# Attention with a local band, then a dense layer: the band mask moved from a product in SBUF to a sum in PSUM, with other joins, costs and a split last store

## The chip, the cores and the metric

The kernel runs on one core of one Trainium2 chip. The metric is the device time of one execution in microseconds (us), the median over several runs. An engine is named as in the profile: PE (TensorE, matmuls), PEld (its weight load, which overlaps PE), DVE (VectorE), ACT (ScalarE), POOL (GpSimd), SP (SyncE, which here only issues DMAs).

## The reference

Eight batches with eight heads, 576 positions, 64 features a head, all float32. Attention has two parts that are added, and its result, 4608 tokens by 512 features, goes through a dense layer with 2048 hidden units.

```python
q_d, k_d, v_d = means of q, k, v over 4 neighbouring positions   # 144 positions
out_up = repeat(softmax(q_d @ k_d.T / 8) @ v_d, 4)               # pooled part
mask = abs(pos[:, None] - pos[None, :]) < 4                      # local part: a band
scores = where(mask, q @ k.T / 8, -1e9)
attn_out = out_up + softmax(scores) @ v
x = attn_out as 4608 x 512
h = x @ w_in                                                     # 512 x 2048
out = (h - tanh(h)) @ w_out                                      # 2048 x 512
```

## The kernel before

**Pairs.** Attention is worked in 32 pairs p of two heads: batch b = p // 4, and j = p % 4 is the place of the pair's 128 features in x. For each pair the chain is:

1. Loads of q and k (`load_qk`, L401) and of v (`load_v`, L426) by SP's queue, into 4 buffers `qkn` and 5 buffers `vst`. A cast of v to bfloat16, `vw` (`prep_v`, L451), and of q and k, `qr` (L515 for p of 4 and more, L523 for the first four).
2. A transpose that brings the features to the partitions: by PE (L547) with copies from PSUM (L551) for pairs 0 to 11, by a DMA of SP (L531) with a copy by ACT (L534) from pair 12 on.
3. Sums over four positions for the pooled part: `half` (L564) and `qkd` (L569) for q and k; for v by matmuls (L492) for the first twelve pairs, by two POOL sums (L472, L476) after that.
4. Scores (L584), into PSUM. A query tile of 120 positions needs 128 keys, so the local scores are 2 heads x 480 columns in two banks, and 2 heads x 96 columns in two others beside the pooled scores (L606). The largest score is not subtracted.
5. Exponentials by ACT from PSUM into the bfloat16 tile `E` in SBUF: 960 columns (L622), 192 (L634), and the pooled 576 (L637).
6. The band. For pairs 0 to 3, PE adds it before the scores: a matmul of the identity with `bias` (L589), which is 0 inside the band and -32768 outside. From pair 4 on DVE multiplies `E` in place, after the exponential, with `mask`, which is 1 inside and 0 outside: 960 columns (L626) and 192 (L641). `mask` is built on POOL; `bias` is made from it by one DVE instruction (L813).
7. Outputs (`outs`, L650 and L657): matmuls of `E` with v, which has a column of ones, so that the sum of the weights comes with it. DVE takes the reciprocal (L670) and scales (L672) into `ln`.
8. Back to features on partitions, with the two parts added. For pairs 0 to 11, matmuls (`back`, L683 to L692) add and transpose at once, and one copy (L720 on DVE or L721 on ACT) gives `xT`. From pair 12 on a DMA of SP transposes `ln` into `lT` (L696), and a `join` of two additions (L703, L709) on DVE or POOL writes `xT`.

**The dense layer** takes 512 tokens at a time, nine blocks kb. `mm1` (L734): 16 x 4 matmuls of 512 columns; ACT takes tanh into `u` (L742) and DVE subtracts it from the PSUM bank into `gT` (L745). `mm2` (L760): 4 token tiles x 16 matmuls, ACT copies to `y` (L771), SP stores (L774). Block 0 does all of mm1, then all of mm2; block 1 does mm1; from block 2 on mm1(kb) alternates with mm2(kb - 1). The weights are loaded, with a cast, in four parts each by POOL's queue (L438 for w_in, L442 for w_out); part f of w_out serves mm2's fc from 4f to 4f + 3. "Dense starts" when x of the first batch, pairs 0 to 3, is there; block 1 needs pairs 4 to 7 too.

**The order.** All instructions are first recorded in class `Program` with a cost in ns. `choice` records one that may go to several engines. `order` (L109 to L222) then simulates the engines: it takes again and again the instruction that can start first, by priority where several can, with the costs given, the times `LAT` from the end of an instruction to its user on another engine, and the PSUM banks (`cap`: how many banks a kind may hold). The result is emitted as it is: each engine runs its list in that order. DMA costs of the simulation are `T_QK`, `T_V`, `T_W`. So a changed cost moves instructions between engines and places, far from the line that was edited. Matmuls of the dense layer fill PE wherever no attention work can run; a few idle fillers (L911) keep PE busy before the dense start.

Of the kernel before, what the change touches and what calls it, by code (L numbers as in the profile page):

```python
# [9 lines left out]
BF16 = mybir.dt.bfloat16  # L10
# [13 lines left out]
class Program:  # L24

    LAT = {"PE": 270, "ACT": 150, "DVE": 110, "POOL": 150, "SP": 50, "DMA": 2200}
    RING = 230

    def __init__(self):
# [8 lines left out]
        self.use = []  # L38
        self.toks = []
# [69 lines left out]
    def order(self):  # L109
# [56 lines left out]
        for i in range(n):  # L166
            if left[i] == 0:
                make_ready(i)
        for step in range(n):
            best = None  # L170
            for eng, cand in ready.items():
                if not cand:
                    continue
                now = max(free.get(eng, 0.0), min(at[i] for i in cand))
                if eng == "PE":
# [5 lines left out]
                elif eng == "DMA":  # L181
                    pick = min((turn.get(self.ring[i][0], -1), start[self.ring[i][1]], i)
                               for i in cand if at[i] <= now)[2]
                else:
                    pick = min((self.ops[i][4], i) for i in cand if at[i] <= now)[1]
# [12 lines left out]
            end = now + self.ops[i][1]  # L198
            want = [t for t in self.use[i] if t.first == i]
# [57 lines left out]
def kernel(  # L257
# [41 lines left out]
    mask = fixed("mask", [128, 576], BF16)  # L299
# [69 lines left out]
    def c_mask():  # L369

        GP.memset(mask, 1.0)
        m4 = mask[:, 0:480].rearrange("p (t c) -> p t c", c=QW)
        for part, pat in ((m4, [[0, 4], [1, QW]]),
                          (mask[:, 480:576], [[1, 96]])):
            neg = [[-s, n] for s, n in pat]
            GP.affine_select(
                out=part, in_=part, compare_op=ALU.is_ge, fill=0.0,
                base=-1, pattern=neg, channel_multiplier=1)
            GP.affine_select(
                out=part, in_=part, compare_op=ALU.is_ge, fill=0.0,  # L380
                base=7, pattern=pat, channel_multiplier=-1)
        GP.affine_select(
            out=mask[:, 0:QW], in_=mask[:, 0:QW], compare_op=ALU.is_ge,
            fill=0.0, base=-4, pattern=[[0, QW]], channel_multiplier=1)
        GP.affine_select(
            out=mask[:, 480:576], in_=mask[:, 480:576], compare_op=ALU.is_ge,
            fill=0.0, base=99, pattern=[[0, 96]], channel_multiplier=-1)
# [115 lines left out]
    def attention(p):  # L503
# [34 lines left out]
        else:  # L538
            for a0, a1, tn, cn in ((0, 5, 290, 740), (5, 9, 230, 620)):
# [10 lines left out]
                def copy(fn, a0=a0, a1=a1, b16=b16):  # L550
# [5 lines left out]
                          ("DVE", cn, lambda copy=copy: copy(V.tensor_copy))][:1 + (p < NP)],  # L556
# [10 lines left out]
        def add2(eng):  # L567
            with nc.allow_low_precision("pooled q and k"):
                eng.tensor_tensor(out=qkd[s][:, 0:G],  # L569
                                  in0=half[:, :, 0, :],  # L570
                                  in1=half[:, :, 1, :], op=ALU.add)
        P.choice([(name, n1, lambda eng=eng: add1(eng)) for name, n1, _, eng in adders],
# [48 lines left out]
        e3 = E[e][:, 1152:1728].rearrange("p (h c) -> p h c", h=2)  # L621
        op("ACT", 960, lambda: A.activation(  # L622
            out=e1, in_=two(t1)[:, :, 0:480], func=AF.Exp, scale=SCALE),
           drain=[t1], writes=[("E", e, 0)], pri=pri)
        if p >= NP:
            op("DVE", 950, lambda: V.tensor_tensor(  # L626
                out=e1, in0=e1,
                in1=mask[:, 0:480].unsqueeze(1).to_broadcast([128, 2, 480]),
                op=ALU.mult), reads=["mask"], writes=[("E", e, 0)], pri=pri)
        yield  # L630
        if not new:
            op("PE", 380 * cold + 100 * (p < NP), s2, slack=late, reads=qks + [("qkd", s)],
               fill=[t2], pri=pri)
        op("ACT", 310, lambda: A.activation(  # L634
# [5 lines left out]
        if p >= NP:  # L640
            op("DVE", 450, lambda: V.tensor_tensor(  # L641
                out=e2v, in0=e2v,
                in1=mask[:, 480:576].unsqueeze(1).to_broadcast([128, 2, 96]),
                op=ALU.mult), reads=["mask"], writes=[("E", e, 1)], pri=pri)
# [50 lines left out]
        if p >= X_DMA:  # L695
# [18 lines left out]
            P.choice([("DVE", 1900, lambda: join(V)), ("POOL", 1400, lambda: join(GP))],  # L714
# [37 lines left out]
    def mm2(kb, i):  # L752
        ts, part, g = i // 4, i % 4, kb % 2
        if part == 0:
            ycur[0] = P.psum(1, "d")
        tok = ycur[0]

        def mm(e):
            for fc in range(4 * part + 2 * e, 4 * part + 2 * e + 2):
                T.matmul(one(tok), gT[g][:, fc, ts * 128:ts * 128 + 128],  # L760
                         w_out_sb[:, fc, :],
                         start=(fc == 0), stop=(fc == N_FF - 1))
        for e in range(2):
            op("PE", 432, lambda e=e: mm(e),
               reads=[("w_out", part, c) for c in range(4)] +
# [179 lines left out]
```

The softmax here doesn't subtract the row's maximum and nothing guards it: scores larger than these inputs give would overflow.

## Time and profile before

| what | value |
|---|---|
| median of 13 runs | 333.79 us (332.4 to 336.17) |
| the profiled execution's own time | 333.7 us |
| its span in the profile | 331.7 us |
| granted clock of TensorE | 1.0 |
| busy: PE, DVE, ACT, POOL | 314.6, 213.2, 202.6, 176.7 us |
| first dense matmul, end of the last one | 25.8, 327.3 us |
| last store: issued, landed | 328.0, 330.05 us |
| a 512-column matmul, one to the next | 0.216 us |
| mask products, 28 + 28 | 32.0 + 16.0 us |
| joins: 9 on DVE, 11 on POOL | 19.8 us, 16.0 us |

The span is what the profile sees of one execution; the time of the execution is 2.0 us longer here. In a list of groups a row has the line, engine, operation, what it writes and reads with shapes, how often, the busy time in all and the mean of one in ns, and then the idle time before it and what ended that. "<-" in the waits names the instruction that released the waiting one. SPq and POOLq are the queues that issue DMAs.

| stretch, us | PE busy | DVE | ACT | POOL |
|---|---|---|---|---|
| 26 to 50 (24) | 22.5 | 19.1 | 17.7 | 11.4 |
| 50 to 100 (50) | 48.8 | 33.7 | 34.8 | 36.1 |
| 100 to 246 (146) | 141.2 | 115.8 | 101.7 | 110.6 |
| 246 to 312 (66) | 65.7 | 26.7 | 28.0 | 1.3 |

After 246 us only the dense layer is left.

### The profile page before, as it was taken

The numbers are of one execution on the slowest core, as the hardware profiler recorded it, in microseconds if no ns is written. First come the engines' busy times: TensorE is split into PE (matmuls) and PEld (weight loads), VectorE is DVE, ScalarE is ACT, GpSimd is POOL, SyncE is SP. The second block draws the span as 40 slices with busy tenths as digits, with TensorE's granted clock in tenths as the row PEclk, the third lists the DMA queues.
The fourth block names the chain that finished last, engine by engine and source line by source line (L and its number), as shares of the span: only waits on it lengthen the run. The fifth ranks groups of instructions, "written<-read, shape, count | busy, mean of one in ns | idle before, by whom it ended". The sixth has DMA issues, their size and how long they took to land.

```text
span 331.7 us, 6505 instructions
## 1 busy us (share of the span) xinstructions
PE 314.6 (95%) x2420; PEld 158.7 (48%) x2461; DVE 213.2 (64%) x330; ACT 202.6 (61%) x334; POOL 176.7 (53%) x211
## 2 busy tenths in 40 slices
PE   7889989999999999999899899999999999999994
PEld 2554445655444444445454345444444444444441
DVE  4877874478966969777979878758754334443300
ACT  3977854589778766687866466868534443344411
POOL 8564547768667698988988848787310000000000
PEclk9999999999999999999999999999999999999999
DMA  7999999999999999999999989982320001000121
GB/s 235 263 224 209 249 236 240 292 296 215 287 218 268 226 185 274 264 235 225 243 243 253 275 212 288 196 199 61 91 59 34 32 35 62 32 32 32 38 90 64
DMA packets 108862, 59.80 MB, mean 180 GB/s; under 512 B 86174, under 2 KB 96030, under 8 KB 108830
## 3 DMA queue, kind: packets, MB, share of 16 engines
q1 hardware_dynamic: 104318, 54.60, 70.7%
q0 software_dynamic: 4224, 4.19, 7.8%
q10 hardware_dynamic: 288, 0.59, 0.5%
q8 instruction: 19, 0.31, 0.4%
q14 instruction: 13, 0.11, 0.1%
HBM read 43.64 MB, written 9.44 MB: 160 GB/s over the span
## 4 chain that ended last, share of the span: by engine, by line
PE 70%; DVE 11%; DMA 9%; ACT 3%; POOL 2%; issue 2%; SPq 1%; POOLq 0%; ACTq 0%; DVEq 0%
PE bank L760 30%; PE bank L734 29%; DMA qkn<-in_k_dram 6%; PE bank L650 2%; DVE E L626 2%; DVE gT L745 2%; PE bank L584 2%; DVE ln L672 2%; PE bank L657 2%; DVE E L641 2%; DVE xT L709 1%; DMA v<-in_v_dram 1%; DMA lT<-ln 1%; ACT E L622 1%; DVE xT L703 1%
## 5 line engine op out<-in xcount | busy, mean ns | idle before, releaser
L734 PE MATMUL bank<-xT,w_in_sb 128*128 128x512 bf16 x557 | 143.7, 379 | 1.4 <-DVE gT L745 0.2
L760 PE MATMUL bank<-w_out_sb,gT 128*128 128x512 bf16 x555 | 141.6, 379 | 1.5 <-issue 0.6
L745 DVE TENSOR_TENSOR gT<-bank,u 128x512 bf16<-128x512 f32 x144 | 97.1, 685 | 62.3 <-ACT u L742 61.7
L742 ACT ACTIVATE u<-bank 128x512 f32<-128x512 f32 x144 | 86.0, 598 | 75.6 <-PE bank L734 74.0
L734 PEld LDWEIGHTS <-w_in_sb 128*128 128x128 bf16 x576 | 53.9, 98 | 62.0 <-issue 0.9
L760 PEld LDWEIGHTS <-gT 128*128 128x128 bf16 x576 | 53.9, 98 | 62.0
L564 POOL TENSOR_TENSOR half<-qk 128x576 f32<-128x576 bf16 x28 | 32.1, 1146 | 20.7 <-ACT qk L551 11.6
L626 DVE TENSOR_TENSOR E<-E,mask 128x960 bf16<-128x960 bf16 x28 | 32.0, 1143 | 12.0 <-ACT E L622 11.9
L622 ACT ACTIVATE E<-bank 128x960 bf16<-128x960 f32 x32 | 31.1, 972 | 12.3 <-PE bank L584 12.1
L515 POOL CAST qr<-qkn 128x1152 bf16<-128x1152 f32 x28 | 32.7, 1168 | 7.9 <-DMA qT<-qr 5.1
L672 DVE TENSOR_TENSOR ln<-bank,r 128x896 bf16<-128x896 f32 x32 | 34.7, 1086 | 0.9
L771 ACT COPY y<-bank 128x512 f32<-128x512 f32 x36 | 21.1, 586 | 19.9 <-PE bank L760 18.3
L451 POOL CAST vw<-vst 128x640 bf16<-128x640 f32 x31 | 25.7, 832 | 9.5 <-DMA vst<-in_v_dram 9.5
L472 POOL TENSOR_TENSOR v<-v 72x512 f32<-72x512 f32 x20 | 25.4, 1272 | 1.6 <-DMA v<-in_v_dram 0.8
L534 ACT COPY qk<-qT 128x1152 bf16<-128x1152 bf16 x20 | 24.1, 1207 | 1.7 <-DMA qT<-qr 1.7
L650 PE MATMUL bank<-vw,E 128*128 128x65 bf16 x320 | 19.8, 194 | 3.2 <-DVE E L641 2.3
L569 POOL TENSOR_TENSOR qkd<-half 128x288 bf16<-128x288 f32 x29 | 21.0, 724 | 1.5 <-DVE r L670 0.5
L476 POOL TENSOR_TENSOR vp<-v 72x256 bf16<-72x256 f32 x20 | 14.5, 725 | 13.6 <-PE bank L657 12.0
L650 PEld LDWEIGHTS <-E 128*128 128x128 bf16 x320 | 16.4, 98 | 10.1 <-DVE E L641 2.5
L637 ACT ACTIVATE E<-bank 128x576 bf16<-128x576 f32 x32 | 21.1, 661 | 0.0
L703 POOL TENSOR_TENSOR xT<-lT 128x480 bf16<-128x480 bf16 x11 | 11.3, 1026 | 14.2 <-DMA lT<-ln 14.1
L641 DVE TENSOR_TENSOR E<-E,mask 128x192 bf16<-128x192 bf16 x28 | 16.0, 571 | 0.8 <-ACT E L634 0.7
(75 smaller groups left out, 223.9 us busy)
## 6 DMA issues: line engine op xcount, KB each, us to landing
vst<-in_v_dram SPq DMA_DIRECT2D x62, 160.0 KB, 4.9
qkn<-in_q_dram SPq DMA_DIRECT2D x32, 288.0 KB, 5.3
out_dram<-y SPq DMA_DIRECT2D x36, 256.0 KB, 4.5
qkn<-in_k_dram SPq DMA_DIRECT2D x30, 288.0 KB, 6.0
v<-in_v_dram SPq DMA_DIRECT2D x20, 288.0 KB
w_in_sb<-in_moe_w_in_dram POOLq DMA_DIRECT2D x4, 512.0 KB, 12.6
w_out_sb<-in_moe_w_out_dram POOLq DMA_DIRECT2D x4, 512.0 KB, 10.8
qkn<-in_k_dram ACTq DMA_DIRECT2D x2, 288.0 KB, 3.4
```

Source lines behind the costliest of these rows:

```text
L451: P.choice([(eng, ns, lambda fn=fn: fn(out=vw[w][:, 2 * jj:2 * jj + 2, :, 0:64], in_=vst[s])) for eng, ns, fn in CAST_V[p >= NEARLY]], rea ...
L472: GP.tensor_tensor(out=v2, in0=v4[s][:, :, :, 0:128], in1=v4[s][:, :, :, 128:256], op=ALU.add)
L515: op("POOL", 1300, lambda: GP.tensor_copy(out=qr[s].rearrange("p a (h d) -> p h a d", h=2), in_=qkn[sn].rearrange("p h (a d) -> p h a d", ...
L564: eng.tensor_tensor(out=half, in0=four[:, :, 0:2, :], in1=four[:, :, 2:4, :], op=ALU.add)
L622: op("ACT", 960, lambda: A.activation(out=e1, in_=two(t1)[:, :, 0:480], func=AF.Exp, scale=SCALE), drain=[t1], writes=[("E", e, 0)], pri=pri)
L626: op("DVE", 950, lambda: V.tensor_tensor(out=e1, in0=e1, in1=mask[:, 0:480].unsqueeze(1).to_broadcast([128, 2, 480]), op=ALU.mult), reads= ...
L650: T.matmul(two(to)[:, hh, 65 * t:65 * t + 65], E[e][:, c:c + 128], vw[w][:, 2 * jj + hh, t, :], start=True, stop=True)
L672: op("DVE", 1060, lambda: V.tensor_tensor(out=ln[s].rearrange("p n (h d) -> p h n d", d=D), in0=blocks()[:, :, :, 0:64], in1=r[s].unsqueez ...
L734: T.matmul(one(tok), w_in_sb[:, dc, fc * 128:(fc + 1) * 128], xT[dc][:, kb * 512:kb * 512 + 512], start=(dc == 0), stop=(dc == N_DC - 1))
L742: op("ACT", 590, lambda: A.activation(out=u[us], in_=one(tok), func=AF.Tanh), drain=[tok], writes=[("u", us)], pri=DPRI)
L745: op("DVE", 670, lambda: V.tensor_tensor(out=gT[g][:, fc, :], in0=one(tok), in1=u[us], op=ALU.subtract), drain=[tok], reads=[("u", us)], w ...
L760: T.matmul(one(tok), gT[g][:, fc, ts * 128:ts * 128 + 128], w_out_sb[:, fc, :], start=(fc == 0), stop=(fc == N_FF - 1))
```

## The change

1. *Band.* `bias` is built on POOL directly; `mask` and the DVE instruction at L813 are gone. For pairs from 4 on DVE adds `bias` to the scores in their PSUM banks, 960 and 192 columns, before the exponentials; the products after them are gone. So the chain scores, exp, mask, outputs becomes scores, band, exp, outputs.
2. *Joins* are on POOL only: 20 pairs there, none on DVE (before 11 and 9).
3. *Order.* The simulation treats POOL and some DVE instructions (the sums `half` and `qkd`) as users of one port, one at a time. Costs change: `LAT` of a DMA, `T_QK`, `T_V`, `T_W`, casts of v (`CAST_V`: from pair 4 on POOL or DVE, before POOL only), `any3`, `ADDERS`, and DVE's copies of q and k. The banks of mm2 are a kind "y" of their own, of which at most 3 are held.
4. *Last store.* The last token tile is worked in two halves of 256 columns: 32 matmuls of 256 columns in place of 16 of 512, two copies, two stores.

In the lists that come out, engine counts move as follows: casts of `vw` from POOL 31 and ACT 1 to POOL 10 and DVE 22; `half` on DVE 4 to 3, `qkd` on DVE 3 to 2, with POOL taking them; first casts of q and k, DVE 1 to 4, POOL 3 to 2, ACT 4 to 2. In the first dense block the attention work of pairs 4 to 11 stands earlier: pair 7's transposes come after 66 dense matmuls, before after 76; the outputs of pair 6 after 82, before 104. The third part of w_out, in the queue of POOL, stands after the `qkd` sum of pair 6; before it stood ahead of that.

```diff
-    LAT = {"PE": 270, "ACT": 150, "DVE": 110, "POOL": 150, "SP": 50, "DMA": 2200}
+    LAT = {"PE": 270, "ACT": 150, "DVE": 110, "POOL": 150, "SP": 50, "DMA": 2000}
...
+        port = 0.0
...
+                if eng == "DVE":
+                    now = max(free.get(eng, 0.0), min(
+                        max(at[i], port) if i in self.port else at[i] for i in cand))
+                elif eng == "POOL":
+                    now = max(now, port)
...
+            if eng == "POOL" or eng == "DVE" and i in self.port:
+                port = end
...
-    def c_mask():
+    def c_bias():
-        GP.memset(mask, 1.0)
+        GP.memset(bias, 0.0)
...
+        P.port.update((len(P.ops), len(P.ops) + 1))
...
+        def band(tok, lo, hi):
+            part = two(tok)[:, :, 0:hi - lo]
+            V.tensor_tensor(out=part, in0=part, in1=bias[:, lo:hi].unsqueeze(1)
+                            .to_broadcast([128, 2, hi - lo]), op=ALU.add)
+        if p >= NP:
+            op("DVE", 1070, lambda: band(t1, 0, 480), reads=["bias"], fill=[t1], pri=pri)
         op("ACT", 960, lambda: A.activation(
             out=e1, in_=two(t1)[:, :, 0:480], func=AF.Exp, scale=SCALE),
            drain=[t1], writes=[("E", e, 0)], pri=pri)
-        if p >= NP:
-            op("DVE", 950, lambda: V.tensor_tensor(
-                out=e1, in0=e1,
-                in1=mask[:, 0:480].unsqueeze(1).to_broadcast([128, 2, 480]),
-                op=ALU.mult), reads=["mask"], writes=[("E", e, 0)], pri=pri)
...
+        if p >= NP:
+            op("DVE", 270, lambda: band(t2, 480, 576), reads=["bias"], fill=[t2], pri=pri)
...
-            P.choice([("DVE", 1900, lambda: join(V)), ("POOL", 1400, lambda: join(GP))],
+            P.choice([("POOL", 1380, lambda: join(GP))],
                      reads=[("lT", s)], writes=[("x", b, j)], pri=pri)
...
-        if part == 0:
-            ycur[0] = P.psum(1, "d")
+        split = kb == NBLK - 1 and ts == 3
+        if split:
+            cols, first, fcs = 256 * (part // 2), part % 2 == 0, 8
+        else:
+            cols, first, fcs = 0, part == 0, 4
+        if first:
+            ycur[0] = P.psum(1, "y")
...
-    T_QK, T_V, T_W, W_PRI, NEARLY = 800, 1000, 2850, 32, NP
-    CAST_V = [[("POOL", 820, GP.tensor_copy), ("ACT", 640, A.copy)],
-              [("POOL", 820, GP.tensor_copy)]]
-    any3 = [("DVE", 700, V.tensor_copy), ("ACT", 650, A.copy),
+    T_QK, T_V, T_W, W_PRI, NEARLY = 760, 850, 3000, 32, NP
+    CAST_V = [[("POOL", 820, GP.tensor_copy), ("ACT", 730, A.copy)],
+              [("POOL", 820, GP.tensor_copy), ("DVE", 760, V.tensor_copy)]]
+    any3 = [("DVE", 750, V.tensor_copy), ("ACT", 670, A.copy),
             ("POOL", 750, GP.tensor_copy)]
     REORDER = [any3, any3]
-    ADDERS = [[("DVE", 700, 420, V), ("POOL", 1150, 750, GP)],
+    ADDERS = [[("DVE", 780, 460, V), ("POOL", 1150, 750, GP)],
               [("POOL", 1150, 750, GP)]]
...
-    op("DVE", 500, lambda: V.tensor_scalar(
-        out=bias, in0=mask, scalar1=-1.0, scalar2=32768.0, op0=ALU.add, op1=ALU.mult),
-       reads=["mask"], writes=["bias"], pri=-94)
...
-    P.cap = {"b": 6, "d": 4}
+    P.cap = {"b": 6, "d": 4, "y": 3}
```

## The prediction

> **What bounds the kernel now.** I read the page's busy times and slices first, then the waits of PE, then the durations of the VectorE (DVE) groups, and last the timeline around the longest waits.
>
> ```profile
> PE 314.6 (95%) x2420; PEld 158.7 (48%) x2461; DVE 213.2 (64%) x330; ACT 202.6 (61%) x334; POOL 176.7 (53%) x211
> ...
> PE   7889989999999999999899899999999999999994
> ```
>
> PE is busy in nearly every slice from the third to the last but one: work taken off DVE pays only where PE stood waiting for it. [...] From the waits of PE between 26 and 332 us (engine, line waited for: total, times, longest, in us):
>
> ```profile
> PE bank L650 <- DVE E L641: 2.3, 2, 1.6
> PE bank L606 <- POOL qkd L569: 1.0, 1, 1.0
> PE bank L760 <- issue: 0.6, 4, 0.2
> PE bank L650 <- DVE E L626: 0.5, 1, 0.5
> PE bank L547 <- POOL qr L515: 0.5, 1, 0.5
> PE bank L650 <- DVE gT L745: 0.4, 1, 0.4
> PE bank L683 <- DVE ln L672: 0.3, 1, 0.3
> ```
>
> Waits for DVE at the output matmuls and before `back` (first, fourth, sixth and seventh line) sum to 2.3 + 0.5 + 0.4 + 0.3 = 3.5 us. The POOL ones, 1.5 us, belong to pair 7 (below). Why is DVE late? Durations of one line each, min/median/max in ns:
>
> ```profile
> L641 DVE TENSOR_TENSOR E<-E,mask x28: 241/250/2796, 29.3 to 240.9; 128x192 bf16<-128x192 bf16 x28
> L626 DVE TENSOR_TENSOR E<-E,mask x28: 640/891/3474, 26.8 to 239.2; 128x960 bf16<-128x960 bf16 x28
> L709 DVE TENSOR_TENSOR xT<-lT x9: 245/716/2907, 111.6 to 236.3; 128x96 bf16<-128x96 bf16 x9
> L745 DVE TENSOR_TENSOR gT<-bank,u x144: 627/691/693, 28.7 to 313.3; 128x512 bf16<-128x512 f32 x144
> ```
>
> The same instruction takes up to eleven times its shortest when both inputs lie in SBUF, and never varies when one is a PSUM bank. The timeline shows when:
>
> ```profile
> 182.85 2.80 DVE L641 TENSOR_TENSOR E<-E,mask 128x192 bf16<-128x192 bf16 x1
> ...
> 183.29 1.14 POOL L515 CAST qr<-qkn 128x1152 bf16<-128x1152 f32 x1
> ...
> 184.39 1.14 POOL L564 TENSOR_TENSOR half<-qk 128x576 f32<-128x576 bf16 x1
> ...
> 185.71 0.20 PE L650 MATMUL bank<-vw,E 128*128 128x65 bf16 x1 [1.59 <-DVE E L641]
> ```
>
> The small mask product ends only when POOL's run of instructions ends, and PE waits 1.59 us for it.
>
> **What the skill says.** The Trainium skill, "SBUF — State Buffer", section "Who interferes with whom": DVE and GpSimd share one port pair under an exclusive lock; a DVE instruction with two SBUF inputs contends with a GpSimd one that reads SBUF, one with at most one SBUF input outside the two-port modes doesn't, and casts can enter those modes. The trace agrees: 241 to 2796 ns for L641, 627 to 693 for L745. "VectorE: DVE Perf Modes", section "The perf-mode tier table", puts a tensor_tensor with a PSUM operand at 1x and an fp32 SBUF copy at up to 2x; L745 has 691 ns for 512 columns, in keeping. "DMA: Bandwidth & Descriptors", section "Queues, rings and completion order", says that each DMA engine alternates between queues that have work; between 18 and 46 us the trace has GpSimd's weight loads at 3.59 MB beside 2.54 MB on SP's queue, so weights do take SP's share.
>
> **The change, part by part.**
>
> *Mask to band.* For pairs 4 to 31, 28 products of 960 and of 192 columns go (32.0 + 16.0 = 48.0 us busy), 28 adds of the same sizes come, read from PSUM and the bias and written to PSUM. No row of before writes PSUM from DVE. From L745 (512 columns, 0.685 us) and L672 (896 columns, 1.086 us): (1.086 - 0.685)/384 = 1.044 ns a column and 0.15 us fixed, so 960 columns take 1.15 and 192 take 0.35 us; 28 x 1.50 = 42.0 us. Bounds: as fast as the unblocked product, 0.64 + 0.24, 24.6 us; twice my estimate if reading and writing PSUM conflict, 84 us, which would bring DVE to 213 - 48 + 84 = 249 us, and in the stretch from 100 to 246 us (115.8 of 146 busy) fill it. I take 1.50 since the nearest rows read PSUM at that rate. The adds have one SBUF input, so nothing on POOL blocks them. On the path: scores, band 1.15, exp 0.97, third exp 0.66, outputs: about 3.8 us where DVE is free, and the order issues 28 dense matmuls (28 x 0.2157 = 6.0 us) between scores and outputs. Covered, unless one L745 (0.69) and one L672 (1.09) and more stand in front. The score banks are held 1.15 us longer; output copies now have their own kind of bank, at most 3, so dense work is not squeezed.
>
> *Joins to POOL.* Nine joins (12.2 + 7.6 = 19.8 us) leave DVE, where nine unblocked ones would take about 8, and POOL gains 9 x (1.03 + 0.43) = 13.1 us. These were the other blocked DVE work, with L745 and the mask of the next pair queued behind. POOL late in the kernel has about 7.0 us of work for each 8.1 us pair.
>
> *Casts of v.* Costs in the planner move 22 of 31 casts of vw (0.83 us on POOL) to DVE: POOL -17.6 us, DVE between 22 x 0.42 and 22 x 0.82, more where POOL holds the port. DVE gets back some of the exposure that it lost: 22 blockable instructions for 56 products and 18 joins. In total POOL falls by some 2 us, DVE by some 7: neither becomes the bound.
>
> So of the 3.5 us, all is removed at the output matmuls. For new waits I charge 1.0 us: the order assumes a DMA 0.2 us shorter and packs tighter, and each cast that blocks for 1 to 3 us stands ahead of L745 and L672. Zero to 3.5 are its ends.
>
> *Order of pairs 4 to 11 in the first dense block.* The new costs pull these earlier. Pair 7's transposes stand after 66 dense matmuls instead of 76. In before they were pinned by its load, not by the order. A piece of the chain of work (start, us, what), and the timeline after it:
>
> ```profile
> 34.79 13.86 DMA qkn<-in_k_dram
> ```
>
> ```profile
> 48.80 1.24 POOL L515 CAST qr<-qkn 128x1152 bf16<-128x1152 f32 x1 [0.50 <-PE bank L606]
> ...
> 50.10 0.68 PE L547 MATMUL bank<-ident,qr 128*128 128x128 bf16 x9 [0.47 <-POOL qr L515]
> ```
>
> Landed at 48.65, cast at 48.80, transposed at 50.10, with 1.5 us of PE waiting. Were the landing unchanged, PE would be ready 10 x 0.2157 + 0.45 (a group of scores that moved too) = 2.6 us earlier and wait that much more: +2.7. Against it: the third w_out load now stands behind a POOL sum, is issued near 42.5 instead of 37.7, and leaves SP's queue alone for some 3 us; while weights flow SP moved 50 to 180 KB a us, alone 230 to 310, so pair 7 can land up to 3 us sooner, which gives 0. Waiting behind the same landing are the DVE casts of v for pairs 5 and 6 (landings 33.48 and 45.64), with L745s behind them; their chain ends at about 50.1 as well. I take +0.8 of 0 to 2.7. The moved w_out load would land near 51 to 52, about as it is needed.
>
> *Last store in halves.* Thirty-two matmuls of 256 columns (0.111 each) for 16 of 512: +0.1. The last copy is 256 columns instead of 512: -0.2 of 0.58. The last store, 2.0 us from issue to landing, carries 128 KB instead of 256: about -0.4, from 0 to -0.8. Together -0.5.
>
> *At no cost:* the tensor_scalar (0.31 us) and the order of constants, behind the first loads before 25.8 us; the planner's port model, which issues nothing.
>
> Sum: -3.5 + 1.0 + 0.8 - 0.5 = -2.2. On the profiled execution, 333.7 (span 331.7), that gives 331.5, span 329.5; the median shown is 333.79, 0.1 above, so 331.6.
>
> **Rivals.**
>
> *The gain is given back (same).* The casts on DVE block as the masks did. For: 22 f32 casts, POOL still busy three quarters of the time from 100 to 246 us (110.6 of 146). Against: v is cast a pair ahead, so a late one holds only the queue behind it. The new waits then are 3.0, not 1.0: 333.6.
>
> *Slower: pair 7 is pulled ahead of its load.* Place: the transposes near 46 to 50 us. Price: the full +2.7; with the casts of v for pair 6 holding the L745s behind them, PE's four "d" banks fill and another 1 to 2 us go there; and as the planner's earlier pairs shift all later ones, some 2 of the 3.5 come back as waits elsewhere. -3.5 + 2.0 + 2.7 + 1.5 - 0.5 = +2.2: 336.0. It decides as soon as pair 7 lands no earlier than about 48.6 and the waits saved later come to less than 2.2 us. For: the trace pins this landing, and nothing in the diff brings loads forward by design. Against: the third w_out load moves away from it.
>
> *Better: the load is early.* Pair 7 lands near 46, its 1.5 us of waits go, no new ones come: -3.5 - 1.5 + 0.3 - 0.5 = -5.2, 328.6.
>
> *The band is slow.* At double price DVE fills and PE waits through 100 to 246 us: above 340.
>
> *The port isn't relieved at all*, should an add in PSUM block too: then as the first rival, 333.6 or more.
>
> **How the numbers follow.** Likeliest case 0.42 (own range 330.3 to 332.9), early load 0.16, given back 0.20 (two thirds of it within 0.3%), pair 7 late 0.18, slow band 0.04. About 0.3%, 1.0 us, is what a measurement of this kernel can tell from no change. Faster: 0.42 + 0.16 = 0.58, and a sixth of given back, 0.03, is 0.61; same 0.14; slower 0.25 from the last cases and a sixth of given back. The range reaches from the early load's middle, 328.8, to most of the late pair, 335.4.
>
> **What would show it.** Right: the adds near 1.15 and 0.35 us with min and max alike; no PE wait on DVE at L650's line; pair 7's transposes before about 48.5 us; the last store landing 1.6 us after issue; DVE about 206 us, POOL about 175. Wrong: a wait of 2 us or more at pair 7's transposes or scores; vw casts on DVE of 2 to 3 us with PE waiting on L745 after them; adds above 1.5 us; PE waiting for POOL's joins or sums.

## The result, and the profile after

The changed kernel takes 337.82 us (median of 11 runs, 335.22 to 338.75) against 333.73 us (48 runs on the same chips): the ratio is 1.0108, 95% interval 1.0079 to 1.0138. It is slower by 1.1%, outside the range that I gave and on the other side. The profiled execution took 335.5 us, span 333.8, in the lower part of its runs; so its waits explain some 2 us of the 4 directly, and the comparisons below carry the rest. Medians here are over all runs of a kernel; the ratios leave out runs that were more than 1.5% longer than its fastest.

The page of the kernel after, busy time and PE's slices:

```profile
PE 314.8 (94%) x2436; PEld 160.9 (48%) x2476; DVE 206.6 (62%) x335; ACT 198.9 (60%) x331; POOL 171.9 (51%) x209
...
PE   6989999999999999989889879899999999999995
```

DVE has 6.6 us less work, POOL 4.8 us less, and PE about the same; yet the end is later. PE's slices show it between the nineteenth and the twenty-seventh, where five of nine are at 7 or 8 tenths, before two. The waits of PE from 26 to 334 us:

```profile
PE bank L742 <- DVE gT L753: 3.4, 3, 1.8
PE bank L594 <- DVE gT L753: 2.6, 5, 0.8
PE bank L742 <- issue: 1.4, 9, 0.2
PE bank L775 <- issue: 0.6, 4, 0.2
PE bank L775 <- DMA w_out_sb<-in_moe_w_out_dram: 0.5, 1, 0.5
PE bank L691 <- DVE ln L680: 0.3, 1, 0.3
```

No wait for DVE is left at the output matmuls (2.3 + 0.5 + 0.4 us before). In this list and the one of before, PE's waits sum to about 9 us against 6, and the last matmul ends at 330.1 us against 327.3. In place of the old waits PE waits 3.4 + 2.6 = 6.0 us for banks that the subtraction (L753, before L745) has not emptied: the first line at the start of dense groups, the second at scores. The subtraction itself takes what it took, 627 to 694 ns. So it starts late. The groups of the band and of the casts of v by shape:

```profile
L634 DVE TENSOR_TENSOR bank<-bank,bias 128x960 f32<-128x960 f32 x28 | 32.4, 1158 | 6.1 <-PE bank L594 6.0
L460 DVE CAST vw<-vst 128x640 bf16<-128x640 f32 x22 | 19.1, 870 | 24.5 <-DMA vst<-in_v_dram 23.6 <-POOL qr L524 0.9
L634 DVE TENSOR_TENSOR bank<-bank,bias 128x192 f32<-128x192 f32 x28 | 10.0, 356 | 1.8 <-PE bank L616 1.8
```

The band costs 1158 and 356 ns and is never blocked. But DVE stands still for 23.6 us before its casts of v, waiting for the load of v. Around the longest of PE's waits the timeline reads:

```profile
197.84 0.60 ACT L750 ACTIVATE u<-bank 128x512 f32<-128x512 f32 x1 [0.28 <-PE bank L742]
...
199.28 0.52 DVE L460 CAST vw<-vst 128x640 bf16<-128x640 f32 x1 [3.51 <-DMA vst<-in_v_dram]
...
199.71 1.87 DVE L753 TENSOR_TENSOR gT<-bank,u 128x512 bf16<-128x512 f32 x3
...
200.44 1.02 PE L742 MATMUL bank<-xT,w_in_sb 128*128 128x512 bf16 x4 [1.83 <-DVE gT L753]
```

The tanh has been ready since 198.44, the cast at the head of DVE's list waits 3.51 us for its load, three subtractions follow it, and PE waits 1.83 us for a bank. The first of the cast's two loads was issued at 194.24 and landed at 198.80. PE has five other places from 140 us on where its waits for the subtraction sum to more than half a microsecond (they end at 143.5, 161.1, 169.1, 185.3 and 209.4). Each has such a cast in front, for which DVE idled 1.9 to 3.3 us. This cast is that of pair 30, whose `ln` ends at 244.35: its outputs are more than 40 us away, and nothing called for doing it then.

### The profile page after: what moved, and what is told of

It reads as the page before. It is cut to its first block, busy times and chain, and to the rows that moved or that the text cites. A ratio compares the mean times of both kernels' runs of the same rounds, so it can differ in the third digit from the quotient of the medians.

```text
span 333.8 us, 6574 instructions
## 1 busy us (share of the span) xinstructions
PE 314.8 (94%) x2436; PEld 160.9 (48%) x2476; DVE 206.6 (62%) x335; ACT 198.9 (60%) x331; POOL 171.9 (51%) x209
## 4 chain that ended last, share of the span: by engine, by line
PE 63%; DMA 17%; POOL 5%; SPq 5%; DVE 5%; issue 3%; ACT 1%; POOLq 0%; DVEq 0%; ACTq 0%
PE bank L742 27%; PE bank L775 26%; DMA vst<-in_v_dram 7%; DMA qkn<-in_k_dram 6%; DMA w_out_sb<-in_moe_w_out_dram 3%; SPq L410 2%; PE bank L594 2%; PE bank L658 2%; DVE ln L680 2%; POOL half L573 1%; DVE vw L460 1%; PE bank L665 1%; DMA lT<-ln 1%; POOL qkd L578 1%; POOL qr L524 1%
## 5 line engine op out<-in xcount | busy, mean ns | idle before, releaser
L775 PE MATMUL bank<-w_out_sb,gT 128*128 128x512 bf16 (+1 forms) x576 | 144.5, 373 | 1.8 <-issue 0.6
L753 DVE TENSOR_TENSOR gT<-bank,u 128x512 bf16<-128x512 f32 x144 | 96.5, 686 | 61.5 <-ACT u L750 60.4
L775 PEld LDWEIGHTS <-gT 128*128 128x128 bf16 x592 | 55.7, 98 | 60.9 <-issue 0.8
L573 POOL TENSOR_TENSOR half<-qk 128x576 f32<-128x576 bf16 x29 | 33.9, 1170 | 24.9 <-ACT qk L560 20.5
L634 DVE TENSOR_TENSOR bank<-bank,bias 128x960 f32<-128x960 f32 (+1 forms) x56 | 40.8, 757 | 7.9 <-PE bank L594 6.0
L524 POOL CAST qr<-qkn 128x1152 bf16<-128x1152 f32 x28 | 32.0, 1143 | 13.5 <-DMA qkn<-in_k_dram 13.3
L460 DVE CAST vw<-vst 128x640 bf16<-128x640 f32 x22 | 19.1, 870 | 24.5 <-DMA vst<-in_v_dram 23.6
L711 POOL TENSOR_TENSOR xT<-lT 128x480 bf16<-128x480 bf16 x20 | 20.7, 1035 | 25.1 <-DMA lT<-ln 25.1
L787 ACT COPY y<-bank 128x512 f32<-128x512 f32 (+1 forms) x37 | 21.1, 570 | 15.3 <-PE bank L775 15.2
L594 PE MATMUL bank<-qk 64*128 64x120 bf16 (+1 forms) x320 | 17.0, 214 | 3.1 <-DVE gT L753 2.6
```

The costliest lines, as they stand in the source:

```text
L524: op("POOL", 1300, lambda: GP.tensor_copy(out=qr[s].rearrange("p a (h d) -> p h a d", h=2), in_=qkn[sn].rearrange("p h (a d) -> p h a d", ...
L573: eng.tensor_tensor(out=half, in0=four[:, :, 0:2, :], in1=four[:, :, 2:4, :], op=ALU.add)
L634: V.tensor_tensor(out=part, in0=part, in1=bias[:, lo:hi].unsqueeze(1) .to_broadcast([128, 2, hi - lo]), op=ALU.add)
L753: op("DVE", 670, lambda: V.tensor_tensor(out=gT[g][:, fc, :], in0=one(tok), in1=u[us], op=ALU.subtract), drain=[tok], reads=[("u", us)], w ...
L775: T.matmul(one(tok)[:, 0:n], gT[g][:, fc, ts * 128:ts * 128 + 128], w_out_sb[:, fc, cols:cols + n], start=(fc == 0), stop=(fc == N_FF - 1))
```

## The experiments

Every ratio is to the kernel before, run on the same chip beside it. Line numbers move by the inserted lines.

**1. The casts on POOL, in the changed kernel's own order.** The edit acts after `order` and before the list is emitted.

```diff
...
+        for p, i in self.cast_v.items():
+            if p >= 12:
+                self.ops[i] = self.alternatives[i]["POOL"] + self.ops[i][3:]
...
```

> The changed kernel with its planned order kept as it is; only the 20 casts of v of pairs 12 to 31 that stand on DVE are issued on POOL instead, at the same place in the list. Theory (a cast on DVE stands in front of the subtractions while its load of v has not landed, PE runs out of banks): the waits of PE for the subtraction's line, 6.0 us in the profile of the changed kernel, fall below 1.5 us; DVE's waiting for the load goes; time near 333 us, 4 to 6 us less than the changed kernel's 337.8. Rival (the band sums hold the score banks longer, the casts have no part in it): the waits stay at 5 to 6 us, time 337 to 338.5. Second rival (POOL with joins and all casts has about 7.9 us of work a pair of 8.1 us and becomes the bound): the waits move to POOL's sums, time 336 or more.

Measured: 333.29 us, ratio 0.9976 (0.9944 to 1.0008). From 1.0108, that is 1.3%, some 4.4 us, for moving casts from one engine to another at the same place. There are 17 of them, not the 20 of the expectation: the plan had the other three on POOL already. On POOL all its 27 casts together wait only 1.9 us for their loads, since POOL comes to them later. PE's waits for the subtraction are gone. What is left is a wait that the changed kernel did not have:

```profile
PE bank L746 <- POOL xT L715: 2.9, 1, 2.9
PE bank L779 <- DMA w_out_sb<-in_moe_w_out_dram: 0.8, 2, 0.5
```

**2. The casts later, still on DVE.** The number 670 is the cost with which the subtraction is recorded; `left` counts four of them.

```diff
...
+        for p, i in self.cast_v.items():
+            if p >= 12 and self.ops[i][0] == "DVE":
+                at = order.index(i)
+                order.pop(at)
+                left = 4
+                while left and order[at] not in users[i]:
+                    left -= self.ops[order[at]][0] == "DVE" and self.ops[order[at]][1] == 670
+                    at += 1
+                order.insert(at, i)
```

> The changed kernel with its planned order kept; each cast of v on DVE of pairs 12 and up is put behind the next four subtractions on DVE, about 7 us later, long before the outputs that need it. The casts stay on DVE. Theory (late load in front of the subtractions): same gain as with the casts on POOL or more, the waits of PE on the subtraction below 1 us, time 331 to 333 us. Rival (the casts' own work on DVE or the port they share with POOL): the casts cost the same later, the waits of PE stay above 4 us, time 336.5 to 338.5.

Measured: 334.58 us, 1.0007 (0.9979 to 1.0035). DVE's idle time for v is 5.7 us instead of 23.6, and PE waits no more for the subtraction:

```profile
L474 DVE CAST vw<-vst 128x640 bf16<-128x640 f32 x22 | 18.2, 826 | 5.7 <-DMA vst<-in_v_dram 5.7
```

So 1.0% of the 1.3% comes back with the same casts on DVE and about the same work (18.2 us against 19.1): it is their place, not their work. Time missed its range (331 to 333): again PE waits, once, for the join of pair 19, here 3.38 us (timeline):

```profile
158.88 1.43 SPq L718 DMA_TRANSPOSE lT<-ln  x1
...
163.53 1.01 POOL L725 TENSOR_TENSOR xT<-lT 128x480 bf16<-128x480 bf16 x1 [1.00 <-DMA lT<-ln]
164.59 0.38 PE L756 MATMUL bank<-xT,w_in_sb 128*128 128x512 bf16 x1 [3.38 <-POOL xT L725]
```

`ln` of pair 19 was ready at 153.72; SP issued its transpose at 158.88, behind loads and other transposes, and it landed near 163.5.

**3. The casts without their loads.** The loads of v from pair 12 on fill four of the five buffers, the casts read the fifth; the values of v there are not the reference's.

```diff
-        t = vst[s]
+        t = vst[s] if p < 12 else vst[p % 4]
...
-            out=vw[w][:, 2 * jj:2 * jj + 2, :, 0:64], in_=vst[s]))
+            out=vw[w][:, 2 * jj:2 * jj + 2, :, 0:64], in_=vst[s if p < 12 else 4]))
```

> The changed kernel with order and engines kept, but the loads of v of pairs 12 and up fill four of the five buffers and the casts read the fifth, which was filled long before: the same transfers and the same casts, and no cast waits for a load (the values of v in those pairs are not the reference's). Theory (late load): the idle time of DVE before its casts, put down to the load of v, falls from 23.6 us to below 3, the waits of PE on the subtraction from 6.0 to below 1 us, span 328.5 to 330.5 against 333.8. Rival (port or work of the casts): the casts still run 0.5 to 2.5 us and the span stays above 332.5.

In one profiled execution the span is 332.7 us. DVE's idle time before the casts is 6.1 us (3.2 of it for loads, of pairs 5 and 6, which the edit leaves alone). PE's waits for the subtraction are gone, as the theory has it. The span is not as it has it: it lies above 332.5, as the rival said, since PE waits 3.3 us for POOL's joins and 2.4 us for `ln`. The casts now run 1070 ns on average, more than with their waits (870); the longest, 2.57 us, has POOL at work beside it all the time. One execution decides here on the waits, not on the time.

**4. The kernel before with its casts on DVE**, in the order of before.

```diff
...
+        for p, i in self.cast_v.items():
+            if p >= 12:
...
+                self.ops[i] = ("DVE", 760, self.dve_cast[p]) + self.ops[i][3:]
...
```

> The kernel before with its planned order kept; only the casts of v of pairs 12 to 31 are issued on DVE in place of POOL, at the same place in the list. Theory (late load in front of the subtractions): DVE idles for loads of v, PE waits for the subtraction by 3 to 7 us more, time 337 to 341 us. Rival (the loss of the changed kernel comes from the band or from its order): time 332 to 335 us.

Measured: 333.29 us, 0.9974 (0.9944 to 1.0004). My expectation of 337 to 341 was wrong. The row of the casts tells why:

```profile
L457 DVE CAST vw<-vst 128x640 bf16<-128x640 f32 x20 | 16.8, 838 | 0.0
```

DVE never waited for v: in that order the casts stood where POOL had come free, later than the landing. So the engine alone does no harm in that order.

**5. The same, casts moved forward** by up to three subtractions, not ahead of the planned transfer.

```diff
...
+                left, low = 3, 1 + max(order.index(d) for d in self.ops[i][3])
+                while left and at > low:
+                    at -= 1
+                    left -= self.ops[order[at]][0] == "DVE" and self.ops[order[at]][1] == 670
+                order.insert(at, i)
```

> The kernel before with its planned order, casts of v of pairs 12 to 31 on DVE as in the earlier run that cost nothing, and now each put up to three subtractions earlier in the list, but not ahead of its load's planned transfer. Theory (not the engine alone, but a place in DVE's list ahead of the landing makes the loss): DVE idles 8 us or more for loads of v, PE waits 3 us or more for the subtraction, time 336.5 to 341 us. Rival (place doesn't matter): 332 to 335 us as without the move.

Measured: 336.37 us, 1.0065 (1.0039 to 1.0092): 0.9% for the move alone. DVE idles 5.5 us for v instead of none, and the casts take 970 ns instead of 838. The time came as expected, at the low end, but not the way: PE waits 3.1 us for mask products (1.7 in experiment 4), which now stood behind the casts, and hardly for the subtraction (0.3). The two profiled executions took the same time, 335.5 us, so these waits do not show where the 0.9% lies.

**6. Only the line of the casts undone**, and the order planned anew.

```diff
-    CAST_V = [[("POOL", 820, GP.tensor_copy), ("ACT", 730, A.copy)],
-              [("POOL", 820, GP.tensor_copy), ("DVE", 760, V.tensor_copy)]]
+    CAST_V = [[("POOL", 820, GP.tensor_copy), ("ACT", 640, A.copy)],
+              [("POOL", 820, GP.tensor_copy)]]
```

> The changed kernel with one line back as before: casts of v from pair 4 on only on POOL (and ACT's cost for the first four as before). The order is planned anew. Theory (the casts on DVE are the loss): PE's waits for the subtraction fall from 6.0 to below 1.5 us, time 332.5 to 334.5 us, within 0.3% of the kernel before or faster, as with the casts on POOL in the old order. Rival (the plan as a whole, not the casts, is worse): 336 us or more, with other waits in place of those.

Measured: 335.09 us, 1.0053 (1.0026 to 1.0081), half of the loss and between the two theories. PE waits 3.4 us for the subtraction though no cast is in front of it:

```profile
149.47 1.18 ACT L543 COPY qk<-qT 128x1152 bf16<-128x1152 bf16 x1 [4.64 <-DMA qT<-qr]
...
150.56 0.59 ACT L750 ACTIVATE u<-bank 128x512 f32<-128x512 f32 x1
151.18 0.69 DVE L753 TENSOR_TENSOR gT<-bank,u 128x512 bf16<-128x512 f32 x1 [4.59 <-ACT u L750]
...
151.93 1.02 PE L775 MATMUL bank<-w_out_sb,gT 128*128 128x512 bf16 x4 [1.95 <-DVE gT L753]
```

At this place, the longest of these waits, it is the same pattern one engine further: on ACT a copy waits 4.64 us for a DMA transpose, the tanh stands behind it, the subtraction waits for the tanh and PE for the subtraction.

**7. The band alone in the kernel before**, the order planned anew.

```diff
+            op("DVE", 1070, lambda: band(t1, 0, 480), reads=["bias"], fill=[t1], pri=pri)
...
-            op("DVE", 950, lambda: V.tensor_tensor(
...
+            op("DVE", 270, lambda: band(t2, 480, 576), reads=["bias"], fill=[t2], pri=pri)
...
-            op("DVE", 450, lambda: V.tensor_tensor(
```

> The kernel before with the band alone: for pairs from 4 on the bias is added in PSUM before the exponential and the products after it are gone; mask and bias are built as before, all costs, joins and the last store as before; the order is planned anew. Theory (the band takes away PE's waits for the mask products, 2.8 us, and at most 3.5 with what stands behind them, and joins on DVE still block): PE's waits for the exponential's mask are gone, waits for loads or joins take some of it, time 331 to 333.5. Rival (the band costs as it holds the score banks 1.2 us longer): time 334.5 or more.

**8. The band and the joins on POOL in the kernel before.**

```diff
-            P.choice([("DVE", 1900, lambda: join(V)), ("POOL", 1400, lambda: join(GP))],
+            P.choice([("POOL", 1400, lambda: join(GP))],
```

> The kernel before with the band and with joins on POOL only; casts of v on POOL, all costs and the last store as before. The band alone gave 342.1 us, with DVE waiting for the transposed result (lT) at its joins and the subtractions queued behind. Theory (whatever waits for a transfer on DVE costs PE): without joins on DVE, PE's waits for the subtraction fall from 7.8 us to below 2 and the time to 333 to 335.5 us. Rival (the band itself is the loss, since it waits on DVE for the scores): 339 us or more.

Measured: 342.07 us, 1.0200 (1.0103 to 1.0296) for the band alone, 333.66 us, 0.9975 (0.9949 to 1.0001) with the joins on POOL. The band alone missed its expectation by far (4 runs). Planned anew it has 14 joins on DVE, where before had 9, and the timeline around its longest wait shows one of them at the head of DVE's list.

```profile
183.07 2.43 DVE L701 TENSOR_TENSOR xT<-lT 128x480 bf16<-128x480 bf16 x1 [2.23 <-DMA lT<-ln]
...
185.43 0.77 DVE L707 TENSOR_TENSOR xT<-lT 128x96 bf16<-128x96 bf16 x1
186.12 1.27 DVE L743 TENSOR_TENSOR gT<-bank,u 128x512 bf16<-128x512 f32 x2
...
186.85 1.44 PE L758 MATMUL bank<-w_out_sb,gT 128*128 128x512 bf16 x3 [3.02 <-DVE gT L743]
```

2.23 us of waiting for the transpose, then 3.2 us of a join that runs beside POOL's work, then the subtraction. Without joins on DVE PE's waits for the subtraction fall from 7.8 to 0.4 us. In these plans band and joins belong together: the pair of them is about 2% faster than the band alone, and level with before or slightly faster. Each plan differs in more places than the joins, so the 2% is not the price of the joins by themselves.

**9. The DMA costs of before in the changed kernel, and 10. the same with late casts.**

```diff
-    LAT = {"PE": 270, "ACT": 150, "DVE": 110, "POOL": 150, "SP": 50, "DMA": 2000}
+    LAT = {"PE": 270, "ACT": 150, "DVE": 110, "POOL": 150, "SP": 50, "DMA": 2200}
...
-    T_QK, T_V, T_W, W_PRI, NEARLY = 760, 850, 3000, 32, NP
+    T_QK, T_V, T_W, W_PRI, NEARLY = 800, 1000, 2850, 32, NP
```

> The changed kernel, planned with the DMA costs of before (latency 2200, 800 for q and k, 1000 for v, 2850 for weights); all else as changed, so the order is planned anew. Theory A (the casts stand before their landing because the new DMA costs promise it too early): DVE's idle time for loads of v falls from 23.6 us to below 8, time 332.5 to 334.5. Theory B (a plan that puts the cast as soon as it believes the data landed is early with either costs, since both are far below the 5.6 us that a load of v takes here): idle time for v stays above 12 us, PE still waits 3 us or more for the subtraction, time 335.5 to 338.5.

> The changed kernel planned with the DMA costs of before, and each cast of v on DVE of pairs 12 and up put behind the next four subtractions. If the order planned with the old costs is the better one and the casts are out of the way: 331 to 333 us, below the kernel before. If the order of the new costs is the better one: no better than the late casts alone, 333.5 to 335.

Measured: 337.93 us, 1.0079 (1.0048 to 1.0110), and 338.66 us, 1.0118 (1.0091 to 1.0144). The old costs don't cure it: theory B holds in time (335.5 to 338.5), though DVE's idle time for v is 8.1 us, below B's 12 (a rough figure: the profiled execution took 341.0 us, 3 us above the median). In that plan the late casts bring nothing, and 338.66 us lies above both ranges of their expectation. PE's waits are spread over DVE's `ln`, ACT's copies and the subtraction (profile with late casts, of an execution 3 us below the median: 2.0 us for the subtraction, 3.0 for ACT's copy to `y`, 1.7 for `ln`). One of its casts runs 1.88 us beside POOL's work, with no load to wait for. What makes this order worse as a whole stays open; a new plan alone can cost as much here as the casts did.

**11. Fewer loads.** The kernel of experiment 2 without the loads for the pooled v from pair 14 on (the sums read old values).

```diff
         def issue():
+            if p >= 14:
+                return
             nc.sync.dma_start(
                 out=v4[s].rearrange("p h w c -> p (h w) c"),
```

> As the kernel with the late casts, but the loads of v for the pooled sums are left out from pair 14 on (the sums read old values): 18 loads of 288 KB less on SP's queue, 5.2 of 60 MB. Theory (with the casts out of the way, the loads and SP's queue set when the join of pair 19 comes, and PE waits 3.4 us for it near 161 us): the join comes 2 us or more earlier, PE's wait for POOL's join falls below 1 us, span 329 to 330.5 against 332.7. Rival (POOL is late with its joins by its own work): the wait stays above 2.5 us, span above 331.5.

In one profiled execution the span is 327.1 us, 5.6 less than with them, more than expected. PE's wait for the join is gone: pair 19's transpose is issued at 153.77, 0.06 us after `ln`, and the join starts at 159.01 (timeline).

```profile
153.77 2.69 SPq L720 DMA_TRANSPOSE lT<-ln  x1
...
159.01 1.01 POOL L727 TENSOR_TENSOR xT<-lT 128x480 bf16<-128x480 bf16 x1 [0.31 <-DMA lT<-ln]
```

So SP's queue with its loads had set that wait, as far as one execution shows. POOL's sums were all still there, and with them the rival that POOL is late by its own work falls.

**12. Fewer loads with nothing left out.** Experiment 6, and the pooled v of pairs 12 to 15 by matmuls, as the kernel does for the first twelve pairs: 4 loads less, 8 POOL sums less, 1.5 us more on PE.

```diff
-    M2_FIRST, T_DMA, X_DMA, NEW, LATE = 16, 12, 12, 12, 0
+    M2_FIRST, T_DMA, X_DMA, NEW, LATE = 16, 12, 12, 16, 0
```

> The changed kernel with casts of v back on POOL, and the pooled v of pairs 12 to 15 by matmuls as for the first twelve pairs: 4 loads of 288 KB less (1.2 MB, about 4.7 us at the 245 GB/s of this stretch), 8 POOL sums less, and 2 x 0.75 us more on PE. Theory (loads pace the join of pair 19, and leaving out 18 of these loads took 5.6 us off the span): PE's wait for the join near 161 us shrinks by 2 us or more, time 331 to 333 us, faster than before by 0.3 to 0.9%. Rival (PE's added work and the new plan eat it): 333.5 to 336 us.

Measured: 328.88 us (328.32 to 329.48, 4 runs), 0.9848 (0.9793 to 0.9904): 1.5% faster than before, beating both kernels. The waits of PE:

```profile
PE bank L742 <- POOL xT L711: 0.8, 1, 0.8
PE bank L742 <- DVE ln L680: 0.3, 1, 0.3
PE bank L742 <- issue: 0.2, 1, 0.2
PE bank L775 <- issue: 0.2, 1, 0.2
```

**13 and 14. Who needs whom.** The same number in the kernel before, and in the changed kernel with its casts on DVE.

> The kernel before with the pooled v of pairs 12 to 15 by matmuls, so 4 loads of 288 KB less and 1.5 us more on PE; mask products, joins and casts as before. If the loads alone set the time, in before as in the changed kernel, it gains as much as the changed one with casts undone did, and gives 328.5 to 330.5 us. If band and joins off DVE are needed for that gain (the mask products and joins on DVE still block and wait): 331.5 to 335 us.

> The changed kernel with the pooled v of pairs 12 to 15 by matmuls, casts of v on DVE as in the change: against the run with casts on POOL and the same lighter loads (328.9 us) only the casts differ. Theory (a cast on DVE ahead of its landing costs with lighter loads too): DVE idles more than 8 us for loads of v, time 331 to 335 us. Rival (the loss was the loads' lateness alone): DVE's idle time for v below 5 us, time 328 to 330.5 us.

Measured: 336.69 us, 1.0106 (1.0009 to 1.0203), in the kernel before (4 runs, one of them 340.7 us): fewer loads alone bring no gain there, with PE waiting 2.4 us for mask products as ever; the time lies above both its ranges. And 336.67 us, 1.0081 (1.0041 to 1.0121), with the casts on DVE: 2.3% more than with them on POOL.

```profile
L460 DVE CAST vw<-vst 128x640 bf16<-128x640 f32 x19 | 18.4, 967 | 21.3 <-DMA vst<-in_v_dram 21.3
```

With lighter loads the casts wait for v nearly as long as in the changed kernel (23.6 us), and the two lines of PE's waits for the subtraction sum to 6.2 us. Among these plans only the one with all three has the gain of experiment 12: band and joins off DVE's way, casts off DVE, fewer loads. Each plan differs as a whole, so the gain isn't shared out among them, and that all three are needed in any plan isn't shown.

**15. The long wait filled.** Experiment 2 with eight useless matmuls ahead of the first of block 4.

```diff
+            if kb == 4 and fc == 0 and part == 0:
+                for _ in range(8):
+                    T.matmul(one(tok), w_in_sb[:, 0, 0:128], w_in_sb[:, 0, 0:512],
+                             start=True, stop=True)
```

> The kernel with the late casts, and eight 512-column matmuls with no use ahead of the first matmul of block 4, where PE waits 3.4 us for pair 19's join: 1.7 us of the wait are filled, 1.7 us remain; no result changes. Theory (after a wait of about 2 us or more PE is granted half the clock for some 3.4 us, so that the wait costs 1.7 us on top of its length): the granted clock stays at 1.0 after 164 us where it was 0.70 and 0.87 in two stretches of 4 us, time 332.3 to 333.7 us, 1 to 2 us less than the 334.6 without. Rival (the clock has no part in it, or falls whatever PE does): no change or up to 1.7 us more, 334.3 to 336.3 us.

After its 3.38 us wait the kernel of experiment 2 has a lower granted clock for two stretches of 4 us (columns: stretch, length, busy PE, PEld, DVE, ACT, POOL with counts, granted clock, DMA share, GB/s):

```profile
160.00:164.00 4.00, 1.22 (x17) 0.58 (x16) 2.67 (x4) 1.20 (x1) 3.00 (x4) 1.00 1.19 242
164.00:168.00 4.00, 3.41 (x11) 1.39 (x11) 0.69 (x1) 2.06 (x3) 3.92 (x6) 0.70 1.02 282
168.00:172.00 4.00, 4.00 (x36) 1.98 (x35) 2.79 (x5) 2.52 (x5) 2.75 (x4) 0.87 1.14 228
```

With the wait filled, the same view of the other kernel:

```profile
164.00:168.00 4.00, 4.00 (x21) 1.78 (x19) 0.69 (x1) 3.35 (x7) 3.60 (x4) 1.00 1.05 283
168.00:172.00 4.00, 3.14 (x39) 1.79 (x39) 3.43 (x7) 2.34 (x4) 3.41 (x5) 1.00 1.08 245
```

The clock's part is real: the mean clock of an execution was 0.995 or below in 17 of 20 runs without the filling and in 1 of 12 with it. The time did not follow: 334.11 us, 1.0000 (0.9968 to 1.0032), against 1.0007; the two intervals do not exclude a gain of 1 us. The profile shows short waits instead between 169 and 174 us (0.24 and 0.40 us at scores, 0.26 and 0.25 at dense groups); whether these are the same load pace catching up again is open.

## Why the prediction was wrong

*Mask to band, right.* 1158 and 356 ns against 1.15 and 0.35 us. The 3.5 us of waits at the output matmuls and before `back` fell to the 0.3 us before `back`. "Nothing on POOL blocks them" holds: the large adds took 1155 to 1167 ns, the small ones 355 to 367. The rule of the shared port in the Trainium skill ("SBUF — State Buffer", section "Who interferes with whom"), by which an add with one SBUF input stays clear of GpSimd and a cast may not, agrees with these and with the casts: 485 to 2565 ns for the same cast on DVE.

*Joins to POOL, right in sign, the size not measured.* I saw DVE relieved of 19.8 us of blocked work, but not that a join on DVE can also make the subtractions wait for a transfer. In before the nine joins waited 1.3 us for theirs; with the band alone, planned anew, fourteen waited 4.9 us, in the plan that lost 2% (experiments 7 and 8). No run moves the joins alone.

*Casts of v, the step that failed.* I charged 1.0 us of new waits, ends 0 to 3.5, priced as blocking at the port; PE's waits for the subtraction were 6.0 us in the profile, and casts on POOL in the same order took 4.4 us off. The cause is not the port but the load: at the six places of PE's waits the cast stands in DVE's list 1.9 to 3.5 us before its data has landed, and everything behind it waits. Of the signs of being wrong, "PE waiting on L745 after them" came, the casts of 2 to 3 us did not: those at the six places ran 0.5 to 1.3 us. The rival "the gain is given back" had the place right, the casts with the subtractions behind them, yet its reason against was my error: that v is cast ahead of its use is true, and it is why the wait was needless, but a wait costs by what stands behind it, not by when its own result is needed.

The profile of before could not show this wait. There POOL waited 9.5 us for v (list of groups), but most of it once, in the first dense block (timeline):

```profile
L451 POOL CAST vw<-vst 128x640 bf16<-128x640 f32 x31 | 25.7, 832 | 9.5 <-DMA vst<-in_v_dram 9.5
```

```profile
45.73 0.72 POOL L451 CAST vw<-vst 128x640 bf16<-128x640 f32 x1 [7.30 <-DMA vst<-in_v_dram]
```

The rest lies before 16 us. After this one, no cast of before waited for its load; put on DVE in the same places, the later ones did not either (experiment 4). The waits came with the places that the new plan chose. It counts on 0.85 us for a load of v and 2.0 us more to its landing (`T_V`, `LAT`), while such a load took 5.6 us from issue to landing (median after). But with the old costs the kernel is as slow (experiment 9), so the changed DMA costs aren't shown to be the reason. And planned anew without casts of v on DVE, the kernel gets back only half of the loss (experiment 6).

*Order of pairs 4 to 11, too dear.* I took +0.8 of 0 to 2.7. Pair 7's cast began at 43.73 as its load landed, its transposes at 46.02, without a wait of PE; before it was 50.10, with 1.5 us of waits. The load came 4.9 us earlier (43.73 against 48.65), as in the rival "the load is early"; the price is 0.5 us of waiting for the third part of w_out, which landed at 49.66. The step gave about -1.0.

*Last store in halves, right.* From the end of the last matmul to the end of the span it is 331.7 - 327.3 = 4.4 us before and 333.8 - 330.1 = 3.7 after, with 0.1 us more of matmuls: -0.6 against -0.5. The traces do not hold the landing of the last store; 330.05 in the table is its issue and the 2.0 us of other stores there.

*What the sum did not hold.* With the casts out of the way these steps should give 3.2 + 1.0 + 0.6 = 4.8 us of gain; experiments 1 and 2 give 0.9976 and 1.0007, that is 0.8 us and none. There the join of pair 19 comes 2.9 to 3.4 us after PE wants it, because SP's queue is behind with loads (experiment 11). So work taken off DVE before 160 us may only let PE arrive sooner at that join; that is argued from these profiles, no run shows it by itself. A lower clock follows the wait (last section). The sum had no term for a join on POOL that PE waits for; it stood only among the signs of being wrong. The slower rival ended near the measured time (336.0), but by pair 7, which was no trouble; so it does not count as foreseen. Of the loss of 1.1%, the casts in their places account for 1.3% by experiment 1, and the rest of the change for about -0.2%, with an interval that includes zero. The rule of the port in the simulation, the banks of kind "y" and the last store were not tested apart.

*Small slips.* The shortest and longest times in the prediction's list differ by nearly twelve, not eleven (2796/241), and L745 varies by a tenth (627 to 693). POOL gives up 21 casts and ACT one, so 17.4 us for POOL's 17.6. None of these moves the sum.

## What to carry to other kernels

On an engine that works its list in order, an instruction that waits for a transfer costs what is queued behind it: before a cast, copy or join is moved to a less busy engine, compare when the new list reaches it with when its transfer lands, by times to landing from a trace, and look who stands behind it in the new place. That it never waited where it was proves nothing: the busy engine may just have come to it late. Do such work on the engine whose queue nobody needs soon, or later in the list, since a result needed 20 us later need not be made at the landing. When removed waits give no gain, look for the next transfer that all have to wait for, and reduce the loads ahead of it.

## What the runs showed of the hardware

A wait of PE can be followed by a lower granted clock. After waits of 1.95 us (experiment 6), 2.9 (experiment 1) and 3.4 us (experiment 2) two stretches of 4 us held a granted clock of 0.64 and 0.94, 0.77 and 0.80, 0.70 and 0.87. Each pair comes to 4 x (0.36 + 0.06), 4 x (0.23 + 0.20) or 4 x (0.30 + 0.13), so 1.7 us of PE work lost, as half the clock for 3.4 us would do. Narrower stretches show the half: 0.50 from 165.7 to 169.0 us in experiment 2, with 1.00 on both sides. The Trainium skill, "TensorE: Matmul & The Clock Gate", section "Part 1: The HAM clock gate", has half the clock after an idle window of about 3.4 us and the return after a busy one as long; the duration agrees, but shorter waits were enough here. Their length alone doesn't decide: in experiment 4 a wait of 1.3 us with one of 0.4 soon after it was followed by a lower clock (0.86 and 0.72), and one of 2.3 us was not; in experiment 5 one of 1.4 us with one of 0.5 was (0.57), and in experiment 3 one of 3.0 us was not. The longest waits in the profiles of before (1.6 us) and after (1.8 us) had none. After the 3.0 us wait of experiment 7 two stretches held 0.55 and 0.60, twice as much: 4 x (0.45 + 0.40) = 3.4 us, a part of it still within the wait. So PE can lose nearly the length of a wait again in work (1.7 us after 1.95), though in experiment 15 saving the clock gave no time that could be measured.
